# Merging the transfers of turned e and of the residual, and a later place in the list for VectorE's work that needs a transfer

## The chip, the cores and the metric

The kernel runs on one core of a Trainium2 chip. A core has five engines with an instruction queue each: TensorE (PE in the profile; PEld is its weight load), VectorE (DVE), ScalarE (ACT), GpSimd (POOL) and SyncE (SP). SyncE computes nothing here: it issues nearly all DMA transfers, one after the other, and sixteen DMA engines carry them out. Every engine takes its own instructions strictly in the order of its queue; between engines there are semaphores. On-chip memory is SBUF (128 partitions); TensorE writes to PSUM.

The metric is the device time of one execution in microseconds (us). The median of three executions before the change is 1267.58 us (1266.56 to 1271.94).

## The reference

Threshold attention over 8 batches and 8 heads, sequence 576, head size 64, followed by a mixer with a token MLP and a channel MLP, all in float32:

```python
scores = scale * np.matmul(q, k.transpose(0, 1, 3, 2))
thresh = np.max(scores, axis=-1, keepdims=True) - tau
scores = np.where(scores >= thresh, scores, -1000000000.0)
attn = np.exp(scores - np.max(scores, axis=-1, keepdims=True))
attn = attn / (np.sum(attn, axis=-1, keepdims=True) + 1e-09)
x = np.matmul(attn, v)                      # heads joined: (8, 576, 512)
h = np.maximum(x.transpose(0, 2, 1) @ w_tok1, 0.0) @ w_tok2
u = x + h.transpose(0, 2, 1)
return u + np.maximum(u @ w_ch1, 0.0) @ w_ch2
```

## The kernel before

**The attention.** A unit is 128 rows of queries for a pair of heads; nine units make up two pairs of heads, and there are 144 units in all. Two units make a round (72 rounds). In a round TensorE makes the scores (L825), VectorE their maxima (L842, `mx`), GpSimd a bias from them (L848), ScalarE masks (L858) and takes exponentials (L868), VectorE adds up and inverts the sums (L276, L277), GpSimd scales (L285, `e`).

**Turning e.** For the product with v the scaled e must be turned. In batch 0 TensorE does it (L300). In the other seven batches (126 units) VectorE turns blocks of 32 by 32 of one unit into a tile `T` (L315), and SyncE then moves the four blocks of 32 partitions of `T` to their places in `eT` with four DMAs of 144 KB, from SBUF to SBUF (`move`, L327). There are three `T` buffers, so a unit can be turned once the moves of the unit three before it have landed. Three units are a group; once a group's `eT` has landed, TensorE multiplies it with v (L365, L370), and the result goes to `xT` (L374). For that product v is loaded by SyncE (L117, L120), and its middle block is split by VectorE (L341, `split_middle`). q and k are loaded by SyncE as well (L106) and turned by VectorE (L269).

**The mixer.** When a batch (a row, in the code) has all its `xT`, its token MLP follows: some x is turned by TensorE (L435), the rest by VectorE and DMAs (`early_x`: L395, L401, moves L406, L412); then come L454 and L472 on TensorE, and VectorE adds (L483). Of the channel MLP, a group of 256 tokens a batch (two in batch 0, none in batch 7) is done between the rounds of the attention: L948 multiplies with w_ch1, ScalarE or VectorE take the ReLU (`g`, L953, L956), L964 multiplies with w_ch2, and VectorE adds the residual into `us` (L978), which SyncE stores (L988). For that the residual is turned first (`turn_u`, L933) into `us`, and moved from there to `ut` by SyncE (`move_u`, L940, eight DMAs a group). There is one `us` buffer: `turn_u` of one batch must wait until the stores of the batch before have landed. What is left of the channel MLP is spilled (L531) and done behind the attention, in a last part with lines from L1264 on, which the change doesn't touch.

**The weights** arrive as 64-bit words and are converted in 31 pieces in turn: loaded by SyncE to one of three raw buffers (L200, `raw_at`), then handled by ScalarE (L215, L217), VectorE (L225, L227, L231) and GpSimd (L239). For the last two pieces the third buffer is not free, since it is the place where they belong, and one of them gets a tile of its own, `spare_a`.

**What sets the order.** The order of every engine's queue up to the last part is made when the program is built, by a list scheduler in the kernel (`Scheduler`). Each operation is put in with an engine, an assumed cost, the operations it depends on and a rank; the scheduler keeps a clock for each engine and takes at each step the operation that can start first, by `start` (L604) and `pick`. For DMAs it assumes an issue time each, a rate and a landing time, and eight in flight (`FLIGHT, RATE, LANDING`). Nothing of these times is in the program: only the order is, and at run time an instruction waits for what it needs, with everything behind it in its queue. TensorE's product banks in PSUM are two, so a product also waits for the copy that empties its bank. A move of `T` enters the list with

```python
key_op("T", u), key_op("V", G - 2) if t % GU == 0 else None    # needs: turned; eT free
dmas=(4, 147, 0.645)                                           # four issues, KB, us each
```

Of the kernel before, what the change touches and what calls it, by code (L numbers as in the profile page):

```python
# [9 lines left out]
F32 = mybir.dt.float32  # L10
# [7 lines left out]
P = 128  # L18
# [3 lines left out]
def kernel(  # L22
# [166 lines left out]
    def load_piece(i):  # L189
        if i >= len(pieces):  # L190
            return
        dst, src = pieces[i]
        rows = dst.shape[0]
        n = 1
        for d in dst.shape[1:]:
            n *= d
        if i == len(pieces) - 2:
            raw_at[i % NRAW] = att.tile([P, 2 * WMAX], U32, tag="spare", bufs=1, name="spare_a")
        raw = raw_at[i % NRAW][0:rows, 0 : n * (2 if wide(i) else 1)].bitcast(src.dtype)
        nc.sync.dma_start(out=like(raw, dst), in_=src)  # L200
# [109 lines left out]
    def turn_blocks(u):  # L310

        b, p0, t = units[u]
        e = st.pop(u)
        T = Ts[u] = att.tile([P, 4, NK * 32], F32, tag="T", bufs=3, name=f"T_{u}")
        nc.vector.transpose(  # L315
            out=T.rearrange("p a (c x) -> p c a x", c=NK), in_=e.rearrange("p (c a x) -> p c a x", c=NK, a=4)
        )

    def move(u):
        b, p0, t = units[u]  # L320
        key, place = (b, p0, t // GU), t % GU
        if place == 0:
            turned_e[key] = att.tile([P, GU, 4, NK * 32], F32, tag="eT", name=f"eT_{u}")
            eTs[key] = turned_e[key].rearrange("p n i (c x) -> p (n i) c x", c=NK)
        T = Ts.pop(u)
        for i in range(4):
            nc.sync.dma_start(  # L327
                out=turned_e[key][:, place, i, :], in_=T[32 * i : 32 * i + 32]
            )

    turned_e = {}

# [213 lines left out]

    TOKEN_RANK, TOKEN_AFTER_TOKEN = 1.5, 2.5
    SLACK, SPARE = 1.0, 4.0
    FLIGHT, RATE, LANDING = 8, 214.0, 1.5
    WARM_UNTIL, WARM_GAP, WARM_TURN = 110.0, 0.6, 0.11  # L550

    class Op:
# [15 lines left out]
    class Scheduler:  # L568
# [33 lines left out]
            return t  # L602

        def start(self, x, eng):  # L604
            t = max([d.landed or d.end + (d.lag if d.eng != eng else 0.0) for d in x.deps] + [0.0])
            if x.dmas and len(self.in_flight) == FLIGHT:
                t = max(t, self.in_flight[0])
            if x.shared and eng == "dve":
                t = max(t, self.clock["pool"])
            if x.bank:  # L610
                frees = [b.free for b in self.banks if b.free is not None]
                if not frees:
                    return None
                t = max(t, min(frees))
            return max(t, self.clock[eng])
# [101 lines left out]


    CONV = len(pieces)
    CR = (1, 1, 2)  # L720
# [54 lines left out]
    def make_pair(n):  # L775
        b, p = pairs[n]
        if n:
            ahead = (key_op("prep", n - 2, 0), key_op("prep", n - 2, 1))
            for lo in range(0, LOADS, 2):
                put(  # L780
                    ("load", n, lo),
                    sched.op(
                        "sp",
                        0.9,
                        lambda lo=lo: load_qk(n, (nc.sync,) * 2, range(lo, lo + 2)),
                        ahead,
                        1 if n >= NP else 0,
                        after=(key_op("load", n - 1, LOADS - 2),),
                        dmas=(2, 107, 0.58),
                    ),  # L790
                )
# [16 lines left out]
        put(("split", n), sched.op("dve" if n >= NP else "pool", 0.25 if n >= NP else 0.5, lambda: split_middle(n), (key_op("loadv", n), free), 2))  # L808


    def scores_of_two(us):
# [107 lines left out]
    def make_groups(b, halves):  # L919
        uT = xTs[b]  # L920
        reads = []
        for i in range(NOW[b]):
# [1 line left out]
            n, nt = GR, GR // P  # L924

            def new_us(s=s, i=i):
                s["us"] = work.tile([P, nt, 4, NCC * 32], F32, tag="us", bufs=1, name=f"us_{b}_{i}")

            def turn_u(s=s, i=i):
                new_us(s)  # L930
                s["ut"] = work.tile([P, nt, 4, NCC * 32], F32, tag="ut", bufs=1, name=f"ut_{b}_{i}")
                for m in range(nt):
                    nc.vector.transpose(  # L933
                        out=s["us"][:, m].rearrange("q a (c d) -> q c a d", c=NCC),
                        in_=uT[:, :, GR * i + P * m : GR * i + P * m + P].rearrange("q c (r a) -> q c a r", a=4),
                    )
# [36 lines left out]
            def leave(bank, t, c, s=s):  # L973
                if not b and "us" not in s:
                    new_us(s)
                o = s["us"][:, t].rearrange("q a x -> q (a x)")[:, P * c : P * c + P]
# [8 lines left out]

            def store(t, s=s, i=i):
                t0 = GR * i + P * t
                nc.sync.dma_start(out=out[b, t0 : t0 + P, :], in_=s["us"][:, t].rearrange("q a x -> q (a x)"))  # L988

            have = halves["20"] + (halves["21"] if i else [])  # L990
            moved = []
            if b:
                turn = sched.op("dve", 1.2, turn_u, have + state["stores"] + state["adds"] + (converted if b == 1 else []), 5)
                reads.append(turn)
                moved = [sched.op("sp", 1.2, lambda k=k, m=move_u: m(k), (turn,), 1, dmas=(nt, 53, 0.645)) for k in range(4)]
            relus = []
            for j in range(NJ):
                x, y = sched.banked(
# [14 lines left out]
            for t in range(nt):  # L1013
# [19 lines left out]
                stores.append(sched.op("sp", 0.35, lambda t=t, f=store: f(t), outs, 2, dmas=(1, 150, 0.35)))  # L1033
            state["ch2"], state["stores"], state["adds"] = seconds, stores, adds
        return reads

# [52 lines left out]
    def make_round(it):  # L1089
# [28 lines left out]
        for u in us:  # L1118
# [4 lines left out]
            if not b:  # L1123
# [15 lines left out]
                if t % GU == GU - 1:  # L1139
# [5 lines left out]
            put(("T", u), sched.op("dve", 1.31, lambda u=u: turn_blocks(u), deps, 4))  # L1145
            put(
                ("M", u),
                sched.op(
                    "sp",
                    2.4,  # L1150
                    lambda u=u: move(u),
                    (key_op("T", u), key_op("V", G - 2) if t % GU == 0 else None),
                    0,
                    after=(key_op("M", u - 1),),
                    dmas=(4, 147, 0.645),
                ),
            )
# [330 lines left out]
```

## Time and profile before

| What | Value |
|---|---|
| median of three executions | 1267.58 us |
| the profiled execution: its own time | 1273.39 us |
| the profiled execution: span from first to last instruction | 1271.4 us |
| TensorE busy | 1237.8 us (97%) |
| VectorE, ScalarE, GpSimd busy | 755.0, 564.0, 315.4 us |
| moves of `T` to `eT` | 504 DMAs, 144 KB each, 3.0 us from issue to landing |
| moves of `us` to `ut` | 128 DMAs of 64 KB, 80 of them in the last part |
| mean granted TensorE clock | 0.991 of full speed |

Times in the profile are counted from the first instruction. The attention with the work between its rounds takes the first 846 us or so, the last part the rest. "SPq" and "DVEq" are the queues (sequencers) of SyncE and VectorE; the time of a DMA issue is the time that SyncE's queue is held by it, not that of the transfer. A busy TensorE includes short waits that the profile's modelled ends hide.

### The profile page before, as it was taken

The page shows a single profiled execution, that of the slowest core. Times are in us where ns is not written, and L with a number is a line of the kernel's source. Part 1 is how long each engine was busy: PE and PEld are TensorE (multiplying, and loading weights), DVE is VectorE, ACT ScalarE, POOL GpSimd, SP SyncE. Part 2 cuts the span into 40 slices and gives each one's busy share as a digit, 9 for nine tenths or more (in the row PEclk, how much of TensorE's full clock was granted, in tenths as well). Part 3 has the DMA queues.
Part 4 walks back from the last instruction along what each step waited for, and adds up shares of the span by engine and source line. Part 5 has one row for each costly group of instructions (what it writes and reads, how often), then busy time and mean ns, then how long its engine had stood idle before and what let it go on. Part 6 is the DMA issues. An engine that isn't in the chain of part 4 may idle for free.

```text
span 1271.4 us, 21773 instructions
## 1 busy us (share of the span) xinstructions
PE 1237.8 (97%) x8150; PEld 1015.3 (80%) x8150; DVE 755.0 (59%) x1163; ACT 564.0 (44%) x1233; POOL 315.4 (25%) x518
## 2 busy tenths in 40 slices
PE   8888999999999999999989999999999999999998
PEld 7656778797678778878867777888988888888887
DVE  6699982656666667756666756761443534444443
ACT  6998862554645545556465455531110202011120
POOL 4565641232223333323323322410001010000100
PEclk9899999999999999999999999999999999999999
DMA  9546985366777786786776875750212101021011
GB/s 167 139 124 166 214 212 131 87 128 160 168 164 175 160 169 150 165 178 137 179 148 135 187 159 111 179 150 1 60 23 67 34 25 42 18 67 25 26 34 33
DMA packets 324216, 149.23 MB, mean 117 GB/s; under 512 B 223696, under 2 KB 316880, under 8 KB 324112
## 3 DMA queue, kind: packets, MB, share of 16 engines
q1 hardware_dynamic: 322240, 147.64, 50.5%
q8 instruction: 64, 1.05, 0.4%
q10 hardware_dynamic: 1872, 0.21, 0.1%
q14 instruction: 40, 0.33, 0.1%
HBM read 47.32 MB, written 13.50 MB: 48 GB/s over the span
## 4 chain that ended last, share of the span: by engine, by line
PE 78%; SPq 6%; DVE 5%; DMA 5%; ACT 4%; issue 2%; POOL 0%; DVEq 0%; ACTq 0%; POOLq 0%
PE bank L964 11%; PE bank L948 10%; PE o L1309 10%; PE sc L825 9%; PE bank L370 7%; PE hx L1309 6%; PE bank L454 5%; PE hmm L1309 4%; PE oz L1309 4%; PE hz L1309 4%; PE bank L472 4%; SPq L327 3%; PE bank L365 2%; DVE mx L842 2%; ACT e L858 2%
## 5 line engine op out<-in xcount | busy, mean ns | idle before, releaser
L285 POOL TENSOR_SCALAR e<-e,rr 128x576 f32<-128x576 f32 x288 | 213.2, 758 | 299.1 <-DVE rr L277 286.6
L858 ACT ACTIVATE e<-sc,bias 128x576 f32<-128x576 f32 x288 | 194.1, 740 | 156.8 <-POOL bias L848 155.1
L842 DVE TENSOR_REDUCE mx<-sc 128x2 f32<-128x1152 f32 x144 | 188.1, 1347 | 58.9 <-PE sc L825 58.4
L868 ACT ACTIVATE e<-e,ntau 128x576 f32<-128x576 f32 x288 | 220.4, 778 | 0.3
L315 DVE STREAM_TRANSPOSE T<-e 128x1152 f32<-128x1152 f32 x126 | 170.0, 1362 | 36.1 <-POOL e L285 22.2
L948 PE MATMUL bank<-xT,wc 128*128 128x256 f32 x768 | 181.0, 389 | 6.1 <-ACT g L953 5.1
L964 PEld LDWEIGHTS bank<-wc,g 128*128 128x128 f32 x1536 | 178.0, 192 | 10.4 <-issue 2.4
L964 PE MATMUL bank<-wc,g 128*128 128x128 f32 x1536 | 181.4, 276 | 0.9 <-DVE xT L483 0.4
L948 PEld LDWEIGHTS bank<-xT,wc 128*128 128x128 f32 x768 | 144.2, 192 | 36.6 <-ACT g L953 6.5
L825 PE MATMUL sc<-kT,qT 64*128 64x192 f32 (+1 forms) x1920 | 168.8, 337 | 2.7 <-ACT e L858 2.7
L825 PEld LDWEIGHTS sc<-kT,qT 64*128 64x128 f32 (+1 forms) x1920 | 140.8, 179 | 32.1 <-issue 16.3
L370 PE MATMUL bank<-eT,lv 128*64 128x384 f32 (+1 forms) x1024 | 135.2, 406 | 0.0
L1392 POOL TENSOR_TENSOR us<-us,ut 128x256 f32<-128x256 f32 x27 | 22.4, 843 | 391.8 <-DVE us L1230 391.8
L370 PEld LDWEIGHTS bank<-eT,lv 128*64 128x64 f32 x1024 | 74.4, 137 | 49.7 <-issue 41.3
L848 POOL TENSOR_SCALAR bias<-mx,toff 128x2 f32<-128x2 f32 x144 | 38.8, 270 | 197.9 <-DVE mx L842 193.3
L454 PE MATMUL bank<-x_sb,w 128*128 128x256 f32 x320 | 72.8, 383 | 0.3 <-DVE eT L305 0.2
L472 PE MATMUL bank<-w,a 128*128 128x192 f32 (+1 forms) x256 | 72.8, 418 | 0.2 <-DVE xT L483 0.2
L454 PEld LDWEIGHTS bank<-x_sb,w 128*128 128x128 f32 x320 | 59.8, 190 | 11.3 <-issue 1.3
L953 ACT ACTIVATE g<-bank 128x256 f32<-128x256 f32 x66 | 25.3, 383 | 92.9 <-PE bank L948 92.7
L1357 ACT ACTIVATE ga<-hmm 128x256 f32<-128x256 f32 x30 | 11.5, 384 | 116.8 <-PE hmm L1309 116.8
L1230 DVE TENSOR_TENSOR temps<-hx,temps 128x256 f32<-128x256 f32 x60 | 25.1, 418 | 56.7 <-PE hx L1309 56.6
L868 ACT ACTIVATION_READ_ACCUMULATOR e<-e,ntau 128x1 f32 x288 | 58.4, 203 | 0.0
(133 smaller groups left out, 1519.6 us busy)
## 6 DMA issues: line engine op xcount, KB each, us to landing
eT<-T SPq DMA_DIRECT2D x504, 144.0 KB, 3.0
lk<-in_k_dram SPq DMA_DIRECT2D x126, 72.0 KB, 2.9
lq<-in_q_dram SPq DMA_DIRECT2D x124, 72.0 KB, 3.1
out_dram<-us SPq DMA_DIRECT2D x32, 256.0 KB, 2.1
ut<-us SPq DMA_DIRECT2D x128, 64.0 KB, 2.1
lv<-in_v_dram SPq DMA_DIRECT2D x112, 72.0 KB, 2.6
spare<-in_moe_w_ch_dram SPq DMA_DIRECT2D x8, 512.0 KB, 3.9
extra<-in_moe_w_ch_dram SPq DMA_DIRECT2D x8, 512.0 KB, 3.8
```

Of the source, the lines that this page charges most:

```text
L285: nc.gpsimd.tensor_scalar(out=eh, in0=eh, scalar1=rr[:, h : h + 1], scalar2=1.0, op0=ALU.mult, op1=ALU.mult)
L315: nc.vector.transpose(out=T.rearrange("p a (c x) -> p c a x", c=NK), in_=e.rearrange("p (c a x) -> p c a x", c=NK, a=4))
L370: nc.tensor.matmul(to[r], lhsT=lv[:, j, :], rhs=e[j], start=False, stop=(c == NI - 1), skip_group_check=True)
L454: nc.tensor.matmul(to, lhsT=w1[:, t, P * m : P * m + P], rhs=x(t), start=(t == 0), stop=(t == NT - 1), skip_group_check=len(products) > 1,)
L472: nc.tensor.matmul(bank[:, n * i : n * i + n], lhsT=hidden[b][:, m, P * c : P * c + P], rhs=w2[:, m, lo : lo + n], start=(m == 0), stop=(m ...
L825: nc.tensor.matmul(sc[h][rows, f, HT * k : HT * k + HT], lhsT=qT[r, cols], rhs=kT[r, HT * f : HT * f + HT], start=True, stop=True, skip_gr ...
L842: nc.vector.tensor_reduce(out=mx[:, h], in_=sc[h][:, :, 0 : 2 * HT].rearrange("p f (k x) -> p k f x", k=2), axis=AX.XY, op=ALU.max)
L858: nc.scalar.activation(out=eh, in_=part[h], func=AF.Prelu, bias=bias[:, h], scale=SCALE, alpha=STEEP)
L868: nc.scalar.activation(out=eh, in_=eh, func=AF.Exp, bias=ntau, accum_out=rs[:, h, 0:1])
L948: nc.tensor.matmul(bank[:, 0:n], lhsT=wc1[:, j, c, :], rhs=uT[:, c, GR * i : GR * i + n], start=(c == 0), stop=(c == NCC - 1))
L964: nc.tensor.matmul(to, lhsT=s["g"][:, j, P * t : P * t + P], rhs=wc2[:, j, P * c : P * c + P], start=(j == 0 and b > 0), stop=(j == NJ - 1 ...
L1309: nc.tensor.matmul(ps, lhsT=l, rhs=r, start=start and x == 0, stop=x == len(pairs) - 1, skip_group_check=not start)
```

## The change

1. **Moves of turned e.** `T` is now a tile for two units, `[P, 4, 2, 288]`, in two buffers (four units) in place of three tiles for one. Where both units of a round belong to one group of three, four DMAs of 288 KB move both at once, after the second of them is turned; where they belong to two groups, each is moved by four DMAs as before. A unit can be turned once the moves of the round two before it have landed.
2. **Moves of the residual.** `us` has its axes in another order, `[P, 4, 2, 128]`: four DMAs in place of eight bring it to `ut`. A store of `us` now reads four runs of 512 bytes in each partition where it read one of 2 KB.
3. **Conversion.** `spare_a` is gone: the last two pieces use the first and the second raw buffer, and their loads are put behind the conversions of pieces 27 and 28.
4. **The list.** In `start`, an operation of VectorE that depends on a transfer is taken to start at the earliest 2.0 us (`LATE`) behind the transfer's assumed landing, once TensorE's clock in the list is past 200 us. Some assumed costs are changed: `turn_u` 1.2 to 2.05, the stores (150 KB, 0.35 us) to (270, 0.55), `split_middle` 0.25 to 0.28, `turn_blocks` 1.31 to 1.3.

```diff
-        if i == len(pieces) - 2:
-            raw_at[i % NRAW] = att.tile([P, 2 * WMAX], U32, tag="spare", bufs=1, name="spare_a")
-        raw = raw_at[i % NRAW][0:rows, 0 : n * (2 if wide(i) else 1)].bitcast(src.dtype)
+        raw = raw_at[(i + (i >= len(pieces) - 2)) % NRAW][0:rows, 0 : n * (2 if wide(i) else 1)].bitcast(src.dtype)
...
-        T = Ts[u] = att.tile([P, 4, NK * 32], F32, tag="T", bufs=3, name=f"T_{u}")
+        if u % 2 == 0 or u - 1 not in Ts:
+            Ts[u - u % 2] = att.tile([P, 4, 2, NK * 32], F32, tag="T", bufs=2, name=f"T_{u}")
         nc.vector.transpose(
-            out=T.rearrange("p a (c x) -> p c a x", c=NK), in_=e.rearrange("p (c a x) -> p c a x", c=NK, a=4)
+            out=Ts[u - u % 2][:, :, u % 2, :].rearrange("p a (c x) -> p c a x", c=NK),
+            in_=e.rearrange("p (c a x) -> p c a x", c=NK, a=4),
         )
...
-        T = Ts.pop(u)
+        T = Ts[us[0] - us[0] % 2]
         for i in range(4):
-            nc.sync.dma_start(
-                out=turned_e[key][:, place, i, :], in_=T[32 * i : 32 * i + 32]
-            )
+            if len(us) == 2:
+                out, rows = turned_e[key][:, place : place + 2, i, :], T[32 * i : 32 * i + 32]
+            else:
+                out, rows = turned_e[key][:, place, i, :], T[32 * i : 32 * i + 32, :, us[0] % 2, :]
+            nc.sync.dma_start(out=out, in_=rows)
...
-    FLIGHT, RATE, LANDING = 8, 214.0, 1.5
+    FLIGHT, RATE, LANDING, LATE, CALM = 8, 214.0, 1.5, 2.0, 200.0
...
-            t = max([d.landed or d.end + (d.lag if d.eng != eng else 0.0) for d in x.deps] + [0.0])
+            late = LATE if eng == "dve" and self.clock["pe"] > CALM else 0.0
+            t = max([d.landed + late if d.landed else d.end + (d.lag if d.eng != eng else 0.0) for d in x.deps] + [0.0])
...
-            put_load(i + NRAW, (key_op("pool", i),))
+            if i + NRAW < CONV - 2:
+                put_load(i + NRAW, (key_op("pool", i),))
+            elif i + NRAW - 1 >= CONV - 2:
+                put_load(i + NRAW - 1, (key_op("pool", i),))
...
             def move_u(k, s=s):
-                for m in range(nt):
-                    nc.sync.dma_start(
-                        out=s["ut"][:, m, k, :], in_=s["us"][32 * k : 32 * k + 32, m]
-                    )
+                nc.sync.dma_start(out=s["ut"][:, :, k, :], in_=s["us"][32 * k : 32 * k + 32])
...
-                nc.sync.dma_start(out=out[b, t0 : t0 + P, :], in_=s["us"][:, t].rearrange("q a x -> q (a x)"))
+                nc.sync.dma_start(out=out[b, t0 : t0 + P, :].rearrange("q (c x) -> q c x", c=NCC), in_=s["us"][:, :, t, :])
...
-                turn = sched.op("dve", 1.2, turn_u, have + state["stores"] + state["adds"] + (converted if b == 1 else []), 5)
+                turn = sched.op("dve", 2.05, turn_u, have + state["stores"] + state["adds"] + (converted if b == 1 else []), 5)
...
-            deps += [key_op("T", u - 1), key_op("M", u - 3)]
...
+            v = u - u % 2
+            deps += [key_op("T", u - 1), key_op("M", v - 4), key_op("M", v - 3)]
...
+        same = units[us[0]][0:2] == units[us[1]][0:2] and units[us[0]][2] // GU == units[us[1]][2] // GU
+        for moved in [us] if same else [us[0:1], us[1:2]]:
...
+                [key_op("T", u) for u in moved] + [key_op("V", G - 2) if t % GU == 0 else None],
+                0,
+                after=(key_op("M", moved[0] - 1),),
+                dmas=(4, 147 * len(moved), 0.67),
```

More of the change, by code (lines that the diff above doesn't have):

```diff
@@ L313, in turn_blocks, with move @@
         e = st.pop(u)
-        T = Ts[u] = att.tile([P, 4, NK * 32], F32, tag="T", bufs=3, name=f"T_{u}")
+        if u % 2 == 0 or u - 1 not in Ts:
+            Ts[u - u % 2] = att.tile([P, 4, 2, NK * 32], F32, tag="T", bufs=2, name=f"T_{u}")
         nc.vector.transpose(
-            out=T.rearrange("p a (c x) -> p c a x", c=NK), in_=e.rearrange("p (c a x) -> p c a x", c=NK, a=4)
-        )
-    def move(u):
-        b, p0, t = units[u]
+            out=Ts[u - u % 2][:, :, u % 2, :].rearrange("p a (c x) -> p c a x", c=NK),
+            in_=e.rearrange("p (c a x) -> p c a x", c=NK, a=4),
+        )
+    def move(us):
+        b, p0, t = units[us[0]]
         key, place = (b, p0, t // GU), t % GU
         if place == 0:
-            turned_e[key] = att.tile([P, GU, 4, NK * 32], F32, tag="eT", name=f"eT_{u}")
+            turned_e[key] = att.tile([P, GU, 4, NK * 32], F32, tag="eT", name=f"eT_{us[0]}")
             eTs[key] = turned_e[key].rearrange("p n i (c x) -> p (n i) c x", c=NK)
-        T = Ts.pop(u)
+        T = Ts[us[0] - us[0] % 2]
         for i in range(4):
-            nc.sync.dma_start(
-                out=turned_e[key][:, place, i, :], in_=T[32 * i : 32 * i + 32]
-            )
+            if len(us) == 2:
[3 more added lines that the diff above has]
+            nc.sync.dma_start(out=out, in_=rows)
     turned_e = {}
@@ L719 @@
     CONV = len(pieces)
+    assert CONV % NRAW == 1
     CR = (1, 1, 2)
@@ L807, in make_pair @@
             put(("loadv", n), sched.op("sp", 2.0, lambda: load_v(n), (free,), 0, after=(key_op("loadv", n - 1),), dmas=(4, 70, 0.67) if n >= NP else (1, 280, 0.5)))
-        put(("split", n), sched.op("dve" if n >= NP else "pool", 0.25 if n >= NP else 0.5, lambda: split_middle(n), (key_op("loadv", n), free), 2))
+        put(("split", n), sched.op("dve" if n >= NP else "pool", 0.28 if n >= NP else 0.5, lambda: split_middle(n), (key_op("loadv", n), free), 2))
     def scores_of_two(us):
@@ L926, in new_us @@
             def new_us(s=s, i=i):
-                s["us"] = work.tile([P, nt, 4, NCC * 32], F32, tag="us", bufs=1, name=f"us_{b}_{i}")
+                s["us"] = work.tile([P, 4, nt, NCC * 32], F32, tag="us", bufs=1, name=f"us_{b}_{i}")
             def turn_u(s=s, i=i):
@@ L933, in turn_u @@
                     nc.vector.transpose(
-                        out=s["us"][:, m].rearrange("q a (c d) -> q c a d", c=NCC),
+                        out=s["us"][:, :, m, :].rearrange("q a (c d) -> q c a d", c=NCC),
                         in_=uT[:, :, GR * i + P * m : GR * i + P * m + P].rearrange("q c (r a) -> q c a r", a=4),
@@ L975, in leave @@
                     new_us(s)
-                o = s["us"][:, t].rearrange("q a x -> q (a x)")[:, P * c : P * c + P]
+                o = s["us"][:, c, t, :]
                 if b:
@@ L992, in make_groups @@
             if b:
-                turn = sched.op("dve", 1.2, turn_u, have + state["stores"] + state["adds"] + (converted if b == 1 else []), 5)
+                turn = sched.op("dve", 2.05, turn_u, have + state["stores"] + state["adds"] + (converted if b == 1 else []), 5)
                 reads.append(turn)
-                moved = [sched.op("sp", 1.2, lambda k=k, m=move_u: m(k), (turn,), 1, dmas=(nt, 53, 0.645)) for k in range(4)]
+                moved = [sched.op("sp", 1.2, lambda k=k, m=move_u: m(k), (turn,), 1, dmas=(1, 107, 0.67)) for k in range(4)]
             relus = []
@@ L1032, in make_groups @@
                 adds += outs
-                stores.append(sched.op("sp", 0.35, lambda t=t, f=store: f(t), outs, 2, dmas=(1, 150, 0.35)))
+                stores.append(sched.op("sp", 0.35, lambda t=t, f=store: f(t), outs, 2, dmas=(1, 270, 0.55)))
             state["ch2"], state["stores"], state["adds"] = seconds, stores, adds
@@ L1143, in make_round @@
                 continue
-            deps += [key_op("T", u - 1), key_op("M", u - 3)]
[L1145 to L1156, printed above, removed]
-            )
+            v = u - u % 2
+            deps += [key_op("T", u - 1), key_op("M", v - 4), key_op("M", v - 3)]
+            put(("T", u), sched.op("dve", 1.3, lambda u=u: turn_blocks(u), deps, 4))
+        if not in_blocks(units[us[0]][0]):
+            return
+        same = units[us[0]][0:2] == units[us[1]][0:2] and units[us[0]][2] // GU == units[us[1]][2] // GU
+        for moved in [us] if same else [us[0:1], us[1:2]]:
+            b, p0, t = units[moved[0]]
+            G = rank_of_group(b, p0, t // GU)
+            x = sched.op(
+                "sp",
+                2.4,
+                lambda moved=moved: move(moved),
+                [key_op("T", u) for u in moved] + [key_op("V", G - 2) if t % GU == 0 else None],
+                0,
+                after=(key_op("M", moved[0] - 1),),
+                dmas=(4, 147 * len(moved), 0.67),
+            )
+            for u in moved:
+                put(("M", u), x)
+            t = units[moved[-1]][2]
             if t % GU == GU - 1:
```

## The prediction

> **What bounds the kernel now.** I cut the span into four stretches with the view of engine time by windows (columns: stretch, its length, busy time of each engine with its number of instructions, granted clock, DMA share, GB/s).
>
> ```profile
> core 0: us, PE busy (x) PEld busy (x) DVE busy (x) ACT busy (x) POOL busy (x), PEclk, DMA share, GB/s
> 0.00:117.00 117.00, 102.41 (x772) 76.69 (x774) 92.99 (x162) 96.90 (x202) 64.23 (x109) 0.94 0.63 142
> 117.00:200.00 83.00, 82.24 (x622) 64.83 (x620) 69.81 (x103) 58.37 (x126) 41.01 (x54) 1.00 0.88 211
> 200.00:846.00 646.00, 633.04 (x4723) 505.01 (x4720) 414.19 (x584) 347.75 (x762) 187.81 (x328) 0.99 0.68 153
> 846.00:1271.40 425.40, 420.16 (x2043) 368.81 (x2041) 178.06 (x316) 60.94 (x145) 22.40 (x27) 1.00 0.14 38
> ```
>
> TensorE is the bound everywhere, and the change takes no work from it. What can be won is its idle time and its clock. The orders of the two programs are the same up to about 117 us, and the last part (from 846 us) is written out by hand and not touched. So the 14.6 us idle of the first stretch stay, and the field is 117 to 846 us: 0.76 + 12.96 = 13.7 us idle. Two slices of 20 us there, from 640 and from 740, have a granted clock of 0.91: 0.09 of 20 us, 1.8 us each, 3.6 together. All that could be won is 17.3 us, 1.4%.
>
> Next, who makes TensorE wait. The view of waits for 117 to 846 us names mostly ScalarE's copies; the chain of waits tells what stands behind them. Around the idle 2.08 us at 746 us it reads (start, length, what):
>
> ```profile
> 733.98 0.61 SPq L327
> ...
> 737.22 2.45 DMA out_dram<-us
> ...
> 740.73 1.06 DVE us L933
> 741.78 1.26 DVE T L315
> 743.04 1.25 DVE mx L842
> ...
> 744.68 1.37 ACT e L858 x2
> 746.05 0.28 ACT g L953
> ...
> 746.38 3.54 PE bank L948 x8
> ```
>
> From the bottom: TensorE waits for a bank, whose ReLU stands behind two masks, these behind a maximum that stands on VectorE behind `turn_u`, which waits for a store; and the store went out late, because SyncE's queue was issuing moves of `T` without a pause. The lines of that queue in order of time (start, time held, line):
>
> ```profile
> 727.59 7.00 SPq L327 DMA_DIRECT2D eT<-T  x8
> 734.69 2.48 SPq L412 DMA_DIRECT2D x_sb<-extra  x4
> 737.22 0.59 SPq L988 DMA_DIRECT2D out_dram<-us  x1
> ```
>
> and of the move's issue from 200 to 846 us (ns min/median/max):
>
> ```profile
> L327 SPq DMA_DIRECT2D eT<-T x440: 542/602/2039, 208.6 to 840.6; - x147
> ```
>
> Such a run of L327 stands in the chain ahead of TensorE's waits at 205 us (1.23 idle), 339 (1.88), 364 (0.99), 641 (2.60) and 746 (2.08); at 444 (0.63) and 545 (0.35) the chain has a v load, of the same queue. Together 9.76 us, plus the 3.6 of clock, as the slices at half clock begin at 641 and 747. The rest, 13.7 - 9.8 = 3.9 us, hangs on copies alone. In 200 to 846 us the queue issues 815 DMAs, held 503 us by them and 0.04 us between two: 537 of 646 us, 83%. In the eleven 20 us slices from 200 to 840 us where the issues take under 16.5 us, TensorE is idle 2.2 us in all; in the 21 others 10.8. What waits directly on transfers is VectorE (us, times, longest):
>
> ```profile
> DVE vl L341 <- DMA lv<-in_v_dram: 29.2, 12, 10.1
> DVE us L933 <- DMA out_dram<-us: 17.4, 5, 6.5
> DVE kT L269 <- DMA lk<-in_k_dram: 12.6, 3, 5.0
> DVE T L315 <- DMA eT<-T: 11.6, 10, 3.6
> ```
>
> **The change part by part.** *Moves of turned e.* Of the 63 rounds, 42 have both units in one group: 42 x 4 + 21 x 8 = 336 issues in place of 504. In 200 to 846 us 440 become 293, 147 fewer. An issue holds the queue 0.60 + 0.04 us. If a merged one costs the same, that is 95 us. No row shows a merged issue. Upper bound: it costs twice as much, and nothing is saved. Lower bound: as one of today. The issue of lk, with 576 runs of 128 bytes, takes 0.50 us (median), less than the 0.60 of this move with 128 runs, so the time doesn't follow the number of runs: I take 0.64, and the queue falls from 83% to (537 - 95 - 14) / 646 = 66%, with the next part.
>
> The bytes stay. In the trace's packet records the 1152-byte packets take 51 ns (median) to 76 ns (mean); a move has 8 on each of 16 engines, 0.4 to 0.6 us, a merged one 0.8 to 1.2. Four merged moves then take 3.3 to 4.9 us of the engines, and land, with the 2.4 us that a move now needs behind its issue (3.0 - 0.6), 5.7 to 7.3 us after the first issue, where a single unit's four took 4 x 0.64 + 2.4 = 5.0. A group that ends in a merged pair waits 0.7 to 2.3 us longer for its last unit, though a pair as a whole (8 x 0.64 + 2.4 = 7.5) doesn't. Queued behind the move are loads and stores; each goes out 2.6 us sooner than behind eight issues. In the order of the new program, the median TensorE work between a group's last move and its first product rises from 4.8 to 7.2 us, which covers it: I take nothing. Where a move now waits for the second turn, SyncE is held for that (1.37 us), with the same loads behind it; that is inside the 2.6. `T`'s wait (11.6 us of VectorE) can only shrink, as the moves it waits for lie as far back or farther.
>
> The Trainium skill ("DMA: Bandwidth & Descriptors", section "Issuing engines are not separate DMA queues") says that the time a sequencer takes to initiate a DMA is usually small relative to the DMA itself. Here the rows disagree: 0.64 us of issue against 0.4 to 0.6 us of the engines. By that rule the merge would free little that matters, and the time would stay near 1267; the second rival below has this as a mechanism.
>
> *Moves and stores of the residual.* 24 issues fewer before 846 us: 24 x 0.64 = 15 us of queue, counted above as 14 with the stores, whose 16 issues may go from 0.50 us to the 0.56 of the spill, the row with 512 runs (L531). A 512-byte packet takes 27 to 35 ns, a 2 KB one 86 to 95: a store takes 32 x 35 = 1.1 us of each engine, against 8 x 95 = 0.8. It lands up to 0.4 us later, on the very chain above: a loss of 0 to 0.4 us at each of two places; I take 0.3 in all.
>
> *Conversion.* The loads of the last two pieces go out one conversion later. One piece's load lands in 3.8 us, and GpSimd's last step takes 1.3. Cover is the channel MLP's first layer: between the last conversion and the first product that needs all of them, the new order has 3.3 us of TensorE's work where it had 1.3. Cost: nothing to 3.8; I take nothing, since the cover grew.
>
> *The list.* 2.0 us of distance moves other VectorE work ahead of what waits for a transfer. Between the last store and the `turn_u` behind it, the old order has 0, 1.4, 4.5, 0, 0 and 0 us of VectorE's work in the six batches (rows' durations, added up along the order), the new one 3.0, 3.6, 7.2, 3.7, 0 and 0. VectorE waited there 1.8, 1.2, 0, 4.0, 4.0 and 6.5 us. The fourth is the stall at 641, which the 3.7 us cover nearly; the fifth, that at 746, gets nothing ahead of it. The last costs TensorE nothing now. Behind the moved work are maxima and turns, and for them TensorE's scores; the list places these with the same clock, so I cost the shift at 0, bounded by 2.0 us for each of the six `turn_u`, 12 us. Some ReLUs and evictions go from VectorE to ScalarE (5 and 6; 0.4 us each); ScalarE is busy 348 of 646 us, so 0.
>
> **The sum.** 9.8 + 3.6 = 13.4 us hang on the queue. I leave the fifth store's stall whole (2.08 + 1.8 = 3.9) and 0.3 for slower stores; the 3.9 us on copies recur in the new order. 13.4 - 3.9 - 0.3 = 9.2 us less. The profiled span of 1271.4 becomes 1262.2, its own time 1273.4 becomes 1264.2. The median lies 5.8 below the latter: 1267.6 - 9.2 = 1258.4, say 1258.
>
> The price of the stall left uses the clock. The gap of 2.60 us at 641 is followed by 3.4 us at half clock, likewise 2.08 at 746. The Trainium skill ("TensorE: Matmul & The Clock Gate", section "HAM oscillation — how this bites in real kernels") puts the limit at idle gaps of about 3.4 us; the trace shows shorter ones do it. By the rule the stall left would cost 2.1, and 3.6 would not have been lost to begin with, so the gain would be 9.8 - 2.1 - 0.3 = 7.4: 1260.
>
> **Rivals.**
>
> *More.* With the queue at 66% all of the field behaves like the eleven slack slices. Without the 1.23 us at 205, whose full queue lies before 200, they have 0.9 us idle in 220, or 2.7 in 646. Then 13.0 - 2.7 + 3.6 = 13.9 go: 1254. For it: that split; against it: the fifth store.
>
> *Nothing: the queue is not it.* The engines carry the same bytes; at 0.68 busy on average and eight transfers in flight, an issue waits for a landing. For it: single issues of up to 2.04 us, and 0.84 DMA share at 360 to 380 us, one of the slices with stalls. Merged moves then hold the queue as long as two did, and only the fourth store's cover counts, 0 to 4.4 (2.60 and 1.8 of clock): 1263 to 1268. Against it: the median issue is 0.602, near the minimum of 0.542; only 32 of the 815 issues exceed 0.9 us.
>
> *Slower: groups wait for their merged pair.* In the new order 8 of 42 groups have under 2.5 us of TensorE's work behind their last move. If each waits the full 2.3 us longer, with none of it planned, that is 18.4 - 9.2 = 9.2 more: 1277. It decides from four such groups (9.2 / 2.3). Against it: the old order has 11 such groups, and only two waits at L365, of 1.88 and 0.99 us, exceed 0.7.
>
> **How the numbers follow.** Forecast 1258: 0.50 (own range 1254 to 1262). More, 1254: 0.15. Nothing, 1263 to 1268: 0.22. Slower, about 1277: 0.13. The range leaves out the last and a little at both ends: 1251 to 1270, the upper end with the 12 us bound of the shift partly in. About 0.5% (6.3 us) is what a measurement of this kernel tells from no change; faster than 1261.2 is "more" and nine tenths of the forecast, 0.60; slower than 1273.9 is the last rival, 0.13, and 0.01 from the bounds; 0.26 between.
>
> **What would show it.** Right: L327's successors have 336 issues near 0.60 us; in 200 to 846 us TensorE is idle 3 to 8 us; no slice at 640 has a clock under 1; the L933 wait falls from 17.4 to about 11 us; waits on lv and lk halve. Wrong: merged issues near 1.2 us, or issues of over 0.9 us far more than 32 (the engines hold them); L365 waiting for `eT` at many groups; idle time before L948 and L454 that has no transfer in its chain, which would mean that the order itself, and not the queue, makes stalls of this size.

## The result: 1.7% slower, and the profile after

| What | Before | After |
|---|---|---|
| median of five executions each, side by side | 1266.56 us (1265.73 to 1271.94) | 1289.22 us (1286.61 to 1289.31) |
| ratio after to before, 95% interval | | 1.0167 [1.0146, 1.0188] |
| span of the profiled execution | 1271.4 us | 1287.4 us |
| TensorE idle, 117 to 846 us | 13.7 us | 28.4 us |
| of it, idle before products of `eT` and v (L365 before, L367 after) | 3.9 us | 22.4 us |
| TensorE time lost to the clock, 117 to 846 us (half the length of its half-clock stretches) | 3.4 us | 8.5 us |
| SyncE, 200 to 846 us: issues, time held by them | 815, 503.0 us | 640, 517.2 us |

The forecast was 1258 us with a range to 1270; the sign was wrong. The span grew by 16.0 us: TensorE's idle time by 13.8 (33.6 to 47.4 us in all) and its busy time by 2.2. Half-clock stretches follow its longer gaps, and one begins inside the gap that ends at 183 us: 1.6 of the 8.5 us lost to the clock fall into idle time (0.1 of 3.4 before), so that without this double count the clock lost 7.0 us where it lost 3.3.

The lines have moved a little: the move of `T` is L331 (L327 before), `turn` of e is L314 (L315), the products with v L367 and L372 (L365, L370), `turn_u` L940 (L933), the middle of v L343 (L341). First the engine time by the same windows (stretch, its length, busy time of each engine with its number of instructions, granted clock, DMA share, GB/s), of after:

```profile
core 0: us, PE busy (x) PEld busy (x) DVE busy (x) ACT busy (x) POOL busy (x), PEclk, DMA share, GB/s
0.00:117.00 117.00, 102.83 (x774) 76.81 (x776) 93.57 (x163) 97.33 (x203) 64.36 (x109) 0.94 0.69 145
117.00:200.00 83.00, 74.37 (x524) 56.86 (x521) 66.64 (x102) 54.88 (x117) 40.25 (x52) 0.96 0.85 197
200.00:846.00 646.00, 626.26 (x4689) 500.75 (x4688) 407.92 (x567) 347.68 (x764) 185.47 (x326) 0.99 0.71 150
846.00:1287.40 441.40, 436.51 (x2173) 384.28 (x2171) 183.81 (x326) 65.88 (x158) 25.33 (x31) 1.00 0.16 42
```

The first stretch is as before, and the last only begins later. The loss is where the merged moves are: idle 0.76 to 8.6 us in the second stretch, 13.0 to 19.7 in the third. The DMA share of the third stretch rose, 0.68 to 0.71, for slightly fewer bytes a second. What TensorE waits for from 117 to 846 us (engine, operation and line, what it waited for: us in all, times, longest):

```profile
PE bank L367 <- DMA eT<-T: 9.2, 2, 6.9
PE bank L367 <- DMA lv<-in_v_dram: 6.1, 3, 3.9
PE bank L367 <- DMA lk<-in_k_dram: 3.8, 1, 3.8
```

Before, a ReLU copy by ScalarE led the same view:

```profile
PE bank L948 <- ACT g L953: 5.1, 3, 2.6
PE bank L365 <- DMA x_sb<-extra: 1.9, 1, 1.9
```

Now three kinds of transfer do, 19.1 us in all, and all three at the same line. The source view of the move (ns min/median/max, first and last start) and, from the view of DMA issues, its two sizes with the median us from issue to landing:

```profile
L331 SPq DMA_DIRECT2D eT<-T x336: 542/627/3063, 122.0 to 858.5; - x168
```

```profile
eT<-T SPq DMA_DIRECT2D x168, 288.0 KB, 5.4
eT<-T SPq DMA_DIRECT2D x168, 144.0 KB, 3.0
```

The median of 627 ns looks as forecast, and hides two kinds of issue. SyncE's queue in order of time at a stall shows them (start, time held):

```profile
348.06 4.93 SPq L331 DMA_DIRECT2D eT<-T  x4
353.04 0.68 SPq L106 DMA_DIRECT2D lq<-in_q_dram  x1
353.76 1.38 SPq L106 DMA_DIRECT2D lk<-in_k_dram  x1
355.24 2.60 SPq L120 DMA_DIRECT2D lv<-in_v_dram  x4
```

Four issues hold the queue 4.93 us, and the chain of waits behind TensorE's idle 3.80 us at 357 us tells them apart (start, length, what):

```profile
348.06 0.64 SPq L331
...
348.74 0.63 SPq L331
...
349.42 1.71 SPq L331
...
351.18 1.82 SPq L331
...
357.23 2.69 DMA lv<-in_v_dram
...
360.04 0.36 DVE vl L343 x2
```

The first two issues are as ever, the third and the fourth are held about 1.7 us each. So it is in nearly all of the 42 merged moves: the four issues last 0.66, 0.78, 1.62 and 1.81 us in the mean (from the trace's issue records), 1.22 us each; the third is over 0.9 us in 38 moves, the fourth in all 42. Behind them v's load is late, then the split of its middle (L343), then TensorE. The longest wait, 6.86 us at 183 us, hangs on the move itself, held in the same way (5.25 us for its four issues), and on a landing of 5.27 us:

```profile
174.79 1.84 SPq L331
...
176.98 0.61 SPq L331
...
177.64 5.27 DMA eT<-T
...
183.04 1.55 PE bank L367 x4
```

VectorE's waits on transfers (us, times, longest):

```profile
DVE vl L343 <- DMA lv<-in_v_dram: 47.4, 13, 11.1
...
DVE us L940 <- DMA out_dram<-us: 3.3, 2, 2.0
```

The split waits 47.4 us where it waited 29.2. `turn_u`, whose wait for a store stood behind the stalls at 641 and 746 us, waits 3.3 where it waited 17.4, and those two stalls are gone.

### The profile page after: what moved, and what is told of

It is laid out like the page before. It is cut to its first block, busy times and chain, and to the rows that moved or that the text cites. A ratio compares the mean times of both kernels' runs of the same rounds, so it can differ in the third digit from the quotient of the medians.

```text
span 1287.4 us, 21416 instructions
## 1 busy us (share of the span) xinstructions
PE 1240.0 (96%) x8150; PEld 1018.7 (79%) x8150; DVE 751.9 (58%) x1156; ACT 565.8 (44%) x1240; POOL 315.4 (24%) x518
## 4 chain that ended last, share of the span: by engine, by line
PE 76%; DVE 8%; SPq 5%; DMA 5%; ACT 3%; issue 2%; POOL 1%; DVEq 0%; ACTq 0%; POOLq 0%
PE bank L968 12%; PE o L1320 10%; PE sc L832 9%; PE bank L952 9%; PE bank L372 7%; PE hx L1320 6%; PE bank L456 5%; PE hz L1320 4%; PE oz L1320 4%; PE hmm L1320 4%; PE bank L474 4%; SPq L331 3%; PE bank L367 2%; DVE mx L849 2%; DMA lv<-in_v_dram 2%
## 5 line engine op out<-in xcount | busy, mean ns | idle before, releaser
L314 DVE STREAM_TRANSPOSE T<-e 128x1152 f32<-128x1152 f32 x126 | 169.9, 1361 | 41.0 <-POOL e L283 29.4
L952 PE MATMUL bank<-xT,wc 128*128 128x256 f32 x768 | 177.4, 385 | 0.2
L832 PEld LDWEIGHTS sc<-kT,qT 64*128 64x128 f32 (+1 forms) x1920 | 141.7, 180 | 33.6 <-issue 17.6
L372 PE MATMUL bank<-eT,lv 128*64 128x384 f32 (+1 forms) x1024 | 139.5, 415 | 0.0
L372 PEld LDWEIGHTS bank<-eT,lv 128*64 128x64 f32 x1024 | 77.3, 140 | 51.9 <-issue 42.9
L1403 POOL TENSOR_TENSOR us<-us,ut 128x256 f32<-128x256 f32 x27 | 22.4, 844 | 389.9 <-DVE us L1241 389.9
L367 PE MATMUL bank<-eT,vl 128*64 128x384 f32 (+1 forms) x256 | 45.7, 435 | 22.8 <-DMA eT<-T 9.2
```

The lines of the kernel that those rows point to most:

```text
L314: nc.vector.transpose(out=Ts[u - u % 2][:, :, u % 2, :].rearrange("p a (c x) -> p c a x", c=NK), in_=e.rearrange("p (c a x) -> p c a x", c ...
L372: nc.tensor.matmul(to[r], lhsT=lv[:, j, :], rhs=e[j], start=False, stop=(c == NI - 1), skip_group_check=True)
L832: nc.tensor.matmul(sc[h][rows, f, HT * k : HT * k + HT], lhsT=qT[r, cols], rhs=kT[r, HT * f : HT * f + HT], start=True, stop=True, skip_gr ...
L952: nc.tensor.matmul(bank[:, 0:n], lhsT=wc1[:, j, c, :], rhs=uT[:, c, GR * i : GR * i + n], start=(c == 0), stop=(c == NCC - 1))
```

## The experiments

The theory after the result: the merged DMA is the loss, since it holds the queue and lands late. Two rivals: the list (another order of VectorE, and an assumed cost of the merged move that is too small), and the residual's merge. Each experiment is compared with the kernel before on the same chip. "Landing" counts from a move's first issue to the completion of its last DMA, the median over the moves, worked out from the trace's records.

### The merged DMA against the list

**e1_split** keeps the list of after, so every engine's order, and splits each merged move into the eight DMAs of before.

```diff
-        for i in range(4):
-            if len(us) == 2:
-                out, rows = turned_e[key][:, place : place + 2, i, :], T[32 * i : 32 * i + 32]
...
+        for j, u in enumerate(us):
+            for i in range(4):
+                nc.sync.dma_start(
+                    out=turned_e[key][:, place + j, i, :], in_=T[32 * i : 32 * i + 32, :, u % 2, :]
+                )
```

> The changed kernel with its list left as it is, but each merged move of two units issued as eight DMAs of 144 KB (unit by unit) at the same place of SyncE's queue. Theory A (the transfer: a merged move takes twice the transfer, its third and fourth issue hold the queue 1.7 us, and its last part lands 8.9 us after its first issue): eight issues hold the queue about 5.2 us, no longer than the four do now (4.9), and land after 7.5; the nine waits at L367 (22 us in all) lose about 1.4 us each, 1276 to 1282 us. Theory B (the list: the 2.0 us and the new order put the work in a worse order, whatever the transfers do): no change, 1286 to 1292.

Measured: 1272.51 us, ratio 1.0022 [1.0003, 1.0040]. With the order unchanged, 1.45 of the 1.67% are back: the merged DMA itself is the cause. Eight single issues hold the queue little longer than four merged ones (4.93 us there); here at the place of the stall shown above:

```profile
342.02 5.15 SPq L328 DMA_DIRECT2D eT<-T  x8
```

They land earlier too: 8.0 us for the last against 8.9, and the first unit of the pair is complete after 5.1. From 117 to 846 us the idle time before products with v falls from 22.4 to 11.1 us; what is left there waits nearly all for v and q (7.1 and 3.1 us in the view of waits). The time came out below the 1276 to 1282 expected: I had counted the earlier landing of the pair, not that of its first unit, which may be the reason but isn't shown to be. In the profiled executions 3.4 us of the difference lie before 117 us as granted clock (6.8 against 3.4 us lost), where the programs don't differ.

**e2_no_merge** makes the list without merged moves and leaves the rest of the change in.

```diff
-        for moved in [us] if same else [us[0:1], us[1:2]]:
+        for moved in [us[0:1], us[1:2]]:
```

> The changed kernel with every unit moved by itself in four DMAs, told so to the list, which is made anew: the 2.0 us, the merged residual, the conversion without its own tile and the T tile for two units stay. Theory A: the loss goes with the merge, 1256 to 1270 us, and the idle time before L367 falls from 22 us to under 6. Theory B: the loss stays, 1280 or more.

Measured: 1268.82 us, 0.9990 [0.9971, 1.0009]. Without the merge, all other parts together neither help nor harm. The idle time before products with v is 5.0 us from 117 to 846 us, nearly all of it one wait at 346 us, for a move of `early_x`.

**e3_honest** leaves the merge in, and tells the list what a merged issue holds.

```diff
-                dmas=(4, 147 * len(moved), 0.67),
+                dmas=(4, 147 * len(moved), 1.2 if len(moved) == 2 else 0.67),
```

> The changed kernel, merged moves and all, but the list is told 1.2 us an issue for a merged move in place of 0.67 (measured: 0.66, 0.78, 1.62, 1.81 for the four). If the loss comes from a list that has SyncE's queue free 2.2 us too early at each of 42 merged moves, it goes when the list knows: 1260 to 1275 us, idle before L367 under 10 us. If merging itself is what costs (first half of a pair lands late whatever is planned), or if the 2.0 us do, it stays over 1280.

Measured: 1282.80 us, 1.0095 [1.0062, 1.0128]. I expected 1260 to 1275: a miss. A list that knows the price takes the idle time before products with v from 22.4 to 9.9 us, but the idle time at all other lines grows from 6.0 to 12.6 us (22.5 in all). The largest part is in this line of the waits of TensorE:

```profile
PE sc L832 <- ACT e L865: 5.6, 2, 5.3
```

So the wrong assumed cost accounts for some 0.7%, and the rest can't be scheduled away by that number.

**e4_late_only** is the kernel before with the two lines of `LATE` alone.

```diff
-    FLIGHT, RATE, LANDING = 8, 214.0, 1.5
+    FLIGHT, RATE, LANDING, LATE, CALM = 8, 214.0, 1.5, 2.0, 200.0
...
-            t = max([d.landed or d.end + (d.lag if d.eng != eng else 0.0) for d in x.deps] + [0.0])
+            late = LATE if eng == "dve" and self.clock["pe"] > CALM else 0.0
+            t = max([d.landed + late if d.landed else d.end + (d.lag if d.eng != eng else 0.0) for d in x.deps] + [0.0])
```

> The kernel before with the 2.0 us for VectorE's work behind a transfer alone. Theory A: not slower than before, 1257 to 1268 us: the wait of L933 for a store falls from 17 us to under 10. Theory B: 1275 or more.

Measured: 1267.61 us, 0.9978 [0.9960, 0.9997]; `turn_u` waits 1.8 us for stores where it waited 17.4. The list is not the loss; alone it gains a little. It could gain more: of the 10.6 us that TensorE is idle from 117 to 846 us here, 7.2 are one wait at L365 for the move of a unit (at 344 us); the longest wait of before at this line is 1.9.

**e9_residual_only** is the kernel before with the residual's merge and its assumed costs alone.

```diff
-                for m in range(nt):
-                    nc.sync.dma_start(
-                        out=s["ut"][:, m, k, :], in_=s["us"][32 * k : 32 * k + 32, m]
-                    )
+                nc.sync.dma_start(out=s["ut"][:, :, k, :], in_=s["us"][32 * k : 32 * k + 32])
```

> The kernel before with the residual's moves merged alone (four DMAs of 128 KB, the stores from runs of 512 bytes, the list told so with the changed kernel's costs). These moves read from 32 partitions too, but there are 24 before 846 us: within 0.5% of before, 1261 to 1274. If merged moves of any kind cost as those of turned e (17 us for 168 of them), 24 would cost 2 to 3 us.

Measured: 1269.77 us, 0.9996 [0.9979, 1.0013]: no change.

### What makes a merged DMA slow

A merged DMA reads 288 KB from 32 partitions. Its four land 4.4, 6.1, 7.0 and 8.9 us after the first issue: one every (8.9 - 4.4) / 3 = 1.5 us, 294,912 B / 1.5 us = 197 GB/s. The single ones of 144 KB land after 2.8, 3.6, 4.1 and 5.1 us, one every 0.78 us, 190 GB/s: the same rate, and only a little slower than the 0.64 us at which SyncE issues them.

The distances between landings are uneven (median distances): 0.83, 0.42 and 0.92 us for the four single DMAs, 1.68, 0.81 and 1.72 for the merged ones. The long ones lie between blocks of the same half of the 128 partitions (0 and 1, 2 and 3), the short one between the halves. Where eight single DMAs follow each other, the next four land 2.67 us after the first four and are issued 2.61 after them: single DMAs keep up with their issue, merged ones don't.

If the 32 partitions set that rate, a DMA of the same size to the same place that reads 128 partitions is faster, and the queue isn't held.

**e7_after_128** is after with the partitions that are read changed, for merged and single moves.

```diff
-                out, rows = turned_e[key][:, place : place + 2, i, :], T[32 * i : 32 * i + 32]
+                out, rows = turned_e[key][:, place : place + 2, i, :], T[:, i, :, :]
...
-                out, rows = turned_e[key][:, place, i, :], T[32 * i : 32 * i + 32, :, us[0] % 2, :]
+                out, rows = turned_e[key][:, place, i, :], T[:, i, us[0] % 2, :]
```

> The changed kernel, list as it is, each DMA of turned e of the same size, with the same runs and the same place to write, but read from all 128 partitions and not from a block of 32 (so eT holds other rows of e: the product with v is another). If reading from 32 partitions is what makes a merged move slow, the third and fourth issue take about 0.65 us instead of 1.7, the last part lands within 6.5 us instead of 8.8, and the time falls below that of the split moves: 1250 to 1270. If its size (256 runs of 1152 bytes) is, nothing changes: 1286 to 1292.

Measured: 1257.92 us, 0.9901 [0.9878, 0.9924]. Its two lines of the view of DMA issues (count, KB, median us to landing), two of its windows, and four merged issues in SyncE's queue:

```profile
eT<-T SPq DMA_DIRECT2D x168, 288.0 KB, 3.2
eT<-T SPq DMA_DIRECT2D x168, 144.0 KB, 2.2
```

```profile
117.00:200.00 83.00, 79.11 (x585) 61.83 (x583) 67.97 (x104) 54.39 (x117) 40.25 (x53) 0.98 0.75 210
200.00:846.00 646.00, 644.25 (x4823) 516.35 (x4820) 422.81 (x581) 355.81 (x783) 188.48 (x330) 1.00 0.57 155
```

```profile
332.88 2.67 SPq L331 DMA_DIRECT2D eT<-T  x4
```

The product with v is of other rows of e here, and in e8 below: the two runs show where the time goes and aren't kernels to keep. A merged DMA lands 3.2 us after its issue, not 5.4; four hold the queue 2.67 us, 0.63 to 0.68 each in the mean over all moves, where a single one takes 0.61; the four land at 2.7, 3.5, 4.5 and 5.5 us, one every 0.93 us, 316 GB/s. In 200 to 846 us the queue is held 413 us of 646, and TensorE is idle 1.75 us. The DMA share is 0.57 where after has 0.71, for no fewer bytes: the packets of 1152 bytes take 55 ns in the mean where after has 84, and so occupy the engines for a shorter time. That is the picture of the forecast. That the time also meets its 1258 is in part luck: beside a before of 1269.2 us it is by the medians 11.3 us less, not 9.2, and the single moves are faster here as well, which the forecast didn't count.

e7 changes one thing more: a row of `T` then stays in its partition, where the kernel moves it to another. The uneven landings above and e5 below, where every row goes where it went, speak for the side that reads; no run here separates the two fully.

**e8_before_128** does the same to the kernel before.

```diff
-                out=turned_e[key][:, place, i, :], in_=T[32 * i : 32 * i + 32]
+                out=turned_e[key][:, place, i, :], in_=T[:, i, :]
```

> The kernel before, list as it is, each DMA of turned e of the same size read from all 128 partitions (so eT holds other rows of e). If the moves of before were held by SyncE's issue (0.64 us each), little changes: eight moves land after 7.5 instead of 7.9 us, 1262 to 1268. If they too were held by the reading side, their landing falls by over 1 us and the time to 1255 to 1262.

Measured: 1267.89 us, 0.9984 [0.9963, 1.0005]. Its DMAs land in 2.1 us against 3.0, and eight of them after 6.7 against 7.9, but the queue is held as long (500.6 us of 646), and the time stays. I had expected this time with a landing that stays, or a landing that falls with a shorter time: neither came whole. So in the kernel before the issues were the limit, as the prediction had it. In after the read rate of 32 partitions is.

**e5_after_0213** changes the order of after's four merged DMAs, so that two in a row don't read the same half of the 128 partitions.

```diff
-        for i in range(4):
+        for i in (0, 2, 1, 3):
```

> The changed kernel, list as it is, the four blocks of partitions moved in the order 0, 2, 1, 3 in place of 0, 1, 2, 3. Theory P: a move from 32 partitions is held back by the side that it reads from, and blocks of different halves of the partitions can go side by side: the last part of a merged move lands after 7 us or less instead of 8.8, and the time falls to 1270 to 1282. Theory Q: one move goes after the other whatever its partitions: landing 8.8 and time 1286 to 1292 as before.

Measured: 1277.90 us, 1.0060 [1.0038, 1.0082], 1.1% of the time back. The four issues last 0.66, 0.73, 1.90 and 0.88 us: the third is still held, the fourth nearly not. They land after 4.4, 5.5, 7.2 and 8.3 us; theory P had 7 or less for the last, so its time came true and its landing in part. From issue to landing:

```profile
eT<-T SPq DMA_DIRECT2D x168, 288.0 KB, 4.8
```

Which 32 partitions are read in turn matters, though the same 128 are written each time: that speaks for a limit where the DMA reads.

The Trainium skill ("SBUF — State Buffer", section "Door 1: The DMA port swizzle (why `[64,N]` ≈ `[32,N]`)") says that partitions 0 to 31, and 0 to 63 as well, reach only 8 of the 16 ports that DMA has to SBUF, and gives 189 GB/s for 32 and 328 GB/s for 128 partitions in transfers of 1 MiB. The runs come near: 190 to 197 GB/s for four in a row, 160 to 178 for two neighbours that read in the same half (144 KB in 0.83 to 0.92 us, 288 KB in 1.68 to 1.72), and 316 GB/s from 128 partitions. The runs' rates are distances between landings of smaller transfers, so how near they come is partly chance. The same page of the Trainium skill, in the section "Can I just issue two DMAs to hit both halves?", answers no, with 6% to be had. Here the alternation gave 8.3 us in place of 8.9 for a move, a gain of that size, but also a fourth issue of 0.88 us in place of 1.81, and 1.1% of the kernel's time.

### What can be kept

| Run | Edit to the kernel before | Median | Ratio [95%] |
|---|---|---|---|
| e6_before_0213 | order 0, 2, 1, 3 | 1266.21 us | 0.9975 [0.9959, 0.9992] |
| e10_late_0213 | that, and `LATE` as in e4 | 1264.14 us | 0.9948 [0.9927, 0.9969] |
| e11_no_merge_0213 | (after:) e2, and that order | 1266.73 us | 0.9976 [0.9960, 0.9992] |
| e12_late_residual_0213 | that order, `LATE`, and the residual as in e9 | 1261.19 us | 0.9929 [0.9902, 0.9955] |

The edit common to all four, in `move`, by itself in e6:

```diff
-        for i in range(4):
+        for i in (0, 2, 1, 3):
```

> The kernel before, list as it is, the four blocks of a unit moved in the order 0, 2, 1, 3. If two moves that read from different halves of the partitions overlap (as the run with merged moves showed), eight moves in a row land after 7.5 us instead of 7.9 and their issue stays at 5.1: same to 0.4% faster, 1263 to 1269 beside a before of about 1269. If the overlap is worth something only where a move is held, no change.

> The kernel before with the 2.0 us in the list and the order 0, 2, 1, 3, nothing merged. The two effects (0.2% for the 2.0 us, 0 to 0.4% for the order) should add: a ratio of 0.994 to 0.998.

> The changed kernel with every unit moved by itself and the order 0, 2, 1, 3: what is left of the change without the merged moves of turned e. A ratio of 0.994 to 1.000 to the kernel before; its wait of 5.0 us at 346 us shrinks if it came from a move.

> The kernel before with the 2.0 us, the order 0, 2, 1, 3 and the residual's moves merged; the three T tiles and the conversion as they were. If the residual's merge frees the queue (24 issues fewer, 15 us), faster than the same without it by up to 2 us: 0.993 to 0.998.

The order of reading and the `LATE` rule gain about a quarter of a per cent each, and add up in e10. In e6 eight DMAs in a row land after 7.8 us, not the 7.5 expected, and a unit's four land 0.71, 0.61 and 0.68 us apart, evenly where before they alternate. In e11 the wait at 346 us, for a move of `early_x`, didn't shrink (5.4 us, 5.0 in e2). e10 has the long wait of e4 as well (7.0 us). e12, whose order of work differs again, doesn't, and beats both kernels: all of the change that doesn't merge moves of `T` or touch the conversion. The first of its windows:

```profile
0.00:117.00 117.00, 101.82 (x808) 75.91 (x810) 95.50 (x167) 100.19 (x210) 66.00 (x110) 0.99 0.67 145
```

From 117 to 846 us TensorE is idle 8.6 us (before 13.7) and loses nothing to the clock (before 3.4). But 5.1 of the 12.7 us by which its span is shorter lie before 117 us, as a clock of 0.99 where before has 0.94; that stretch doesn't differ between the programs, and in other executions its clock varied likewise. Whether e12 is better than e10 the intervals don't tell.

## Why the prediction was wrong

- **What bounds the kernel: right in part.** With the queue held 413 us instead of 503 (e7), TensorE's idle time in 117 to 846 us falls from 13.7 to 5.6 us, and the clock's loss from 3.4 to 1.7. But e12 comes to 8.6 us with the queue held 496 us, e2 to 10.6 with 499: a good part of what the forecast put down to a full queue goes with another order of work alone.
- **The price of a merged issue: the step that failed first.** "No row shows a merged issue ... I take 0.64", with twice as much as the upper bound. It is 1.22 us in the mean of a move's four, nearly that bound, and the prediction's first sign of being wrong. The 95 us of queue that 147 fewer issues were to free did not come: the moves' issues hold it 265 us where they held it 275, and SyncE is held 517 us in all where it was 503, since loads behind a held move are held as well (mean of lv 0.65 to 0.77 us, of lk 0.58 to 0.69). The argument for 0.64, that lk with 576 runs issues faster than a move with 128, ruled out one reason for a longer issue and not the one at work, how fast reads of 32 partitions land.
- **The transfer of a merged DMA: wrong with it.** 0.8 to 1.2 us each, from packet durations over 16 engines; measured 1.5. A move lands 8.9 us after its first issue, not 5.7 to 7.3. The single moves showed it already, with 0.83 to 0.92 us between the landings of two blocks of the same half, had I taken it from their landings and not from the packets.
- **"Which covers it: I take nothing": wrong by that.** The longer wait was to be covered by TensorE's work behind the last move. With 3.9 us more landing than a single unit has, and loads behind a held move that are held themselves, cover ran out: 22.4 us idle before the products with v where there were 3.9. The view of waits puts 19.1 us of it, at six places, down to transfers. The rival "Slower: groups wait for their merged pair" had 18.4 us of such waits at eight groups and 1277 us, with a chance of 0.13. That the products lost 18.5 us more is a match by chance: only 9.2 of the 19.1 us, at two places, wait for `eT`; the other 9.9 wait for loads of v and k behind moves, which that rival didn't have. It also counted on 9.2 us of gain elsewhere; 3.8 us of other idle time went, and the clock lost 3.7 us more outside the idle time. The span of 1287.4 stands against 1271.4 in an execution of before that was itself 5.8 us above the median.
- **The rival "Nothing: merged moves hold the queue as long as two": its mechanism is what happened**, 4.9 us against 5.1. It lacked the late landing, which turned no gain into a loss. I held against it that only 32 of 815 issues exceeded 0.9 us; of the 128 of 640 after, 83 are moves of `T`, mostly third and fourth issues of merged ones, and the rest mostly loads behind them. Single DMAs of before, which land as fast as they are issued, couldn't show it.
- **The list and the stores: better than forecast.** `turn_u` waits 3.3 us, not the 11 expected, and both stalls of 641 and 746 us are gone. e4 puts the gain of the rule at 0.2%.
- **Residual and conversion: as forecast in time.** e9 shows no change for the first, and e2, which holds both, none either. A store of `us` between the rounds lands 0.1 us later (median of sixteen, 3.25 against 3.18), within the bound of 0.4. The conversion was not tried by itself.
- **The clock: as forecast in kind.** Stretches at half clock follow the longer gaps: in after 6.83 us from 180 us on, and 3.41 us at each of 357, 463 and 566.

Where a merged DMA costs about what I took, the time is near the 1258 of the forecast (e7, 1257.92); but each block of the turned e has to come from its own 32 partitions.

## What to carry to other kernels

Before merging DMAs to save issues, take the rate of the transfers from landings in a row, and compare it with the issue rate: here four landed one every 0.78 us and were issued one every 0.64, so that larger ones only moved the wait into the queue, and the first unit of a pair landed later than before. Look at the distances one by one: a mean over blocks of both halves of the partitions hides that two of the same half stand in each other's way. A median over issues hides this; look at the issues of one burst by their place. Where blocks of few partitions are read one after the other, an order that alternates between the halves of the partitions costs nothing to try.

## What the runs showed of the hardware

- An issue on SyncE's queue can be held while earlier DMAs are outstanding. Of four reads of 288 KB from 32 partitions each, the first two issues take 0.63 us and the next two 1.7 and 1.8 (medians); of four from 128 partitions, with as many bytes, all take 0.62 to 0.63. So the bytes issued don't decide alone. What does (a queue of each DMA engine, a port) these runs leave open.
- DMAs within SBUF that read 32 partitions each land at 190 to 197 GB/s when four follow each other, at 160 to 178 from one to the next within the same half of the partitions; from 128 partitions it is 316 GB/s, into the same 128 partitions.
- The length of a gap doesn't decide alone whether half clock follows: in after, 2.32 us idle at 342 us was not followed by it, 1.90 us at 462 us was. The records of the clock show why. Its changes lie on a grid of 3.413 us (within one execution their distances are multiples of it, to about 1 ns), and what counts is how long TensorE is idle within one interval of the grid. The 2.32 us fall into two intervals, 0.75 and 1.57; the 1.90 us lie in one. In the fourteen traces, from 70 to 1250 us, 4800 intervals were at full clock: all 25 with 1.92 us of idle time or more were followed by half clock, none of the 4772 with 1.88 or less, and one of the three between (1.904 us yes; 1.896 and 1.914 no). So a wait of 2 us costs clock or not by where it falls.
